# Rows of w_out kept in fours on a partition, and every fourth column of w_in as weights

## The chip, the cores and the metric

The kernel runs on one core of a Trainium2 chip. What counts is the device time of one execution in microseconds. The kernel before takes 178.99 us (median of three runs, 178.23 to 181.95).

## What is computed

A gated linear attention over 4 batches and 8 heads of 48 columns, 768 steps long, feeds a two-layer feed-forward block. Cut to what matters:

```python
f = 1.0 / (1.0 + np.exp(-f_logit))
for t in range(S):
    state = f[:, :, t, :, None] * state + np.einsum('bhd,bhe->bhde', k[:, :, t], v[:, :, t])
    y[:, :, t] = np.einsum('bhd,bhde->bhe', q[:, :, t], state)
x = y.transpose(0, 2, 1, 3).reshape(B * S, H * D)     # 3072 tokens of 384
h = x @ w_in                                          # 384 x 2048
g = h * (1.0 / (1.0 + np.exp(-h)))
out = g @ w_out                                       # 2048 x 384
```

All inputs and the output are float32. The sum over the 2048 columns of `h` may be taken in any order, as long as column f of `w_in` meets row f of `w_out`.

## The kernel before

The sequence is cut into chunks of 128 steps; two chunks (two batches, or two neighbouring chunks of one batch) form a pair, and there are 12 pairs. For each pair the kernel computes the attention inside the chunks and the running state in bfloat16, transposes the result into `xT` (384 rows on three blocks of 128 partitions, 256 tokens), and puts it through the block.

The first product (`mi`, L237 to L246) makes `h` with the hidden columns on partitions. One step `mi.P.j` fills one PSUM buffer of 128 x 512 with two blocks n = 2j and 2j+1 of 128 hidden columns for 256 tokens. Each block is three matmuls, one for each 128 rows of `w_in`: the weights are `w_in_sb[:, kk, n*128:(n+1)*128]`, 128 x 128, the moving operand is 256 columns of `xT`. A weight load and a matmul are two instructions on TensorE. In all L244 issues 576 pairs. The silu (`si`, L249, on ACT) writes the two blocks into `hT[:, 2j:2j+2, :]`. The second product (`mo`, L279) takes `hT[:, n, tokens]` as weights and `w_out_sb[:, n, :]` (384 columns) as the moving operand and sums over the 16 blocks n; `mo.P.i.s` does four of them. There are 384 such pairs.

Both weight matrices are loaded once, by four DMAs each, and turned to bfloat16 on the way (L197 to L206). They are issued by POOL, from its own queue. `wi.n` brings columns 512n to 512n+511 of `w_in`, that is blocks 4n to 4n+3, in rows of 2048 B. `wo.n` brings rows 512n to 512n+511 of `w_out`: partition p gets rows 512n + p, + 128, + 256 and + 384, each a row of 1536 B.

The order is written out by hand. `PLAN` lists every step with its engine and its buffers, and each engine runs its steps in that order; waits between engines, and between DMAs and engines, are put in by the framework, from the regions that an instruction reads and writes. The plan begins with `idle.512.10` and `idle.256.1`: ten matmuls of 512 columns and one of 256 that compute nothing (L424). The four w_in loads stand in the order `wi.1`, `wi.3`, `wi.0`, `wi.2`, then come `wo.0` to `wo.3`, each between other steps of POOL. The steps of TensorE around the first product's beginning, in order: `d.0` (L270), `mi.1.2`, `mi.1.3` (blocks 4 to 7), `y.0` (L258), `yi.0.1` (L352), `mi.1.6` (blocks 12, 13), `yT.0.0` and `yT.0.1` (L364), then 13 more `mi` steps of six matmuls, then the second product. The loads of q, k, v and f_logit, the DMA transposes and most stores are on SP's queue.

Of the kernel before, what the change touches and what calls it, by code (L numbers as in the profile page):

```python
# [106 lines left out]
def kernel(  # L107
# [10 lines left out]
    nc = tc.nc  # L118
# [8 lines left out]
    NT = d_ff // 128  # L127
# [28 lines left out]
    w_in_sb = sb.tile([128, KT, d_ff], BF16, name="w_in_sb")  # L156
    w_out_sb = sb.tile([128, NT, d_model], BF16, name="w_out_sb")
    w_in_src = moe_w_in.rearrange("(ko ki) n -> ki ko n", ki=128)
    w_out_src = moe_w_out.rearrange("(ko ki) n -> ki ko n", ki=128)
    SRC = {"f": f_logit, "k": k, "q": q, "v": v}  # L160

    plan = []
# [12 lines left out]
    at = lambda *key: where[key]  # L175
# [21 lines left out]
    def emit(kind, rest, eng):  # L197
        if kind in ("wi", "wo"):
            n, parts = rest[0], count[kind]
            if kind == "wi":  # L200
                w = d_ff // parts
                nc.gpsimd.dma_start(out=w_in_sb[:, :, n * w:(n + 1) * w], in_=w_in_src[:, :, n * w:(n + 1) * w])
            else:
                w = NT // parts
                nc.gpsimd.dma_start(out=w_out_sb[:, n * w:(n + 1) * w, :], in_=w_out_src[:, n * w:(n + 1) * w, :])
            return  # L206
        P = rest[0]
        form, *us = PAIRS[P]
        T = form == "T"
        if kind in SRC:  # L210
            j, parts = rest[1], count[kind, P]
            (b, c), (b1, c1) = us
            if T:
                h = H // parts
                w = h * 2 * D
                src = SRC[kind][b, j * h:(j + 1) * h, c * C:(c + 2) * C].rearrange("h (p t) d -> p h (t d)", t=2)
                dst = at(kind, P)[:, j * w:(j + 1) * w].rearrange("p (h w) -> p h w", h=h)
            else:
                n = 2 // parts
                w = n * HD  # L220
# [3 lines left out]
        if kind in "EL":  # L224
            j, parts = rest[1], count[kind, P]
            w = 2 * HD // parts
# [4 lines left out]
            if T:  # L231
                h = H // parts
                return nc.scalar.activation(lf.rearrange("p j h d -> p h j d")[:, j * h:(j + 1) * h, :, 0:D],
                                            e.rearrange("p (h j d) -> p h j d", j=2, d=D), AF.Ln, bias=1.0)
            n = 2 // parts
            return nc.scalar.activation(lf[:, j * n:(j + 1) * n, :, 0:D], e.rearrange("p (i h d) -> p i h d", i=n, d=D), AF.Ln, bias=1.0)
        if kind == "mi":  # L237
            j = rest[1]
            h = at("h", P, j).rearrange("p (n c) -> p n c", n=2)
            for i in range(2):  # L240
                n = 2 * j + i
                cols = slice(rest[2] * C, (rest[2] + 1) * C) if len(rest) > 2 else slice(0, 2 * C)
                for kk in range(KT):
                    nc.tensor.matmul(h[:, i, cols], w_in_sb[:, kk, n * 128:(n + 1) * 128], at("xT", P)[:, kk, cols],  # L244
                                     start=(kk == 0), stop=(kk == KT - 1))
            return  # L246
        if kind == "si":
# [25 lines left out]
        i = rest[1]  # L273
# [67 lines left out]
        elif kind == "at":  # L341
            r = rest[2]
# [78 lines left out]
    def run(kind, rest, eng, got):  # L421
        if kind == "idle":
            for _ in range(rest[1]):
                nc.tensor.matmul(buf["pb", int(got)][:, 0:rest[0]], triu, zero[:, 0:rest[0]], start=True, stop=True, skip_group_check=True)  # L424
            return
        slots = iter(got.split(",") if got else [])
        for key in takes(kind, rest):
            if key not in where:
                cls = cls_of(key[0])
                if cls == "st":  # L430
                    cls = f"st{PAIRS[key[1]][1 + key[2]][0]}"
                elif cls == "qkT" and len(key) == 2:
                    cls = "qkTT"
                where[key] = buf[cls, int(next(slots))]
        assert next(slots, None) is None, (kind, rest, got)
        emit(kind, rest, eng)
# [69 lines left out]
```

## Time and profile before

| | us |
|---|---|
| median of three runs | 178.99 (178.23 to 181.95) |
| the profiled execution | 178.94 |
| its span, first to last instruction | 177.2 |
| ACT's silu, L249, 96 of 610 ns | 50.5 busy |
| POOL's state update, L383, 40 of 543 ns | 21.7 busy |

The page counts an engine busy from the start of an instruction to its end; overlapping instructions are counted once. TensorE's matmuls are pipelined, so the spacing of their starts, and not the length of one, is what they cost in a stream. "PEld" are the weight loads, which overlap the matmuls. The granted clock, "PEclk", is 1.000 for the whole span. The 16 DMA engines moved 32.12 MB, at a mean of 181 GB/s; of the DMA engines' time SP's queue took 76.2% and POOL's 12.2%.

### The profile page before, as it was taken

What the parts mean: (1) busy time and instruction counts of PE and PEld (TensorE: products, weight loads), DVE (VectorE), ACT (ScalarE), POOL (GpSimd) and SP (SyncE); (2) the same over time, 40 slices, a digit from 0 to 9 for tenths busy, and PEclk for the clock granted to TensorE, in tenths of its full rate; (3) what the DMA queues carried; (4) which work ended last, traced back from release to release, by engine and by line L of the source; (5) the groups of instructions that cost most, each with busy time, mean ns of one, the idle gap of its engine ahead of it and who ended that gap; (6) DMA issues with size and microseconds to landing.
All of it is one profiled execution on the core that took longest, in us unless ns stands there. A gap on an engine that the chain in (4) does not pass through costs nothing.

```text
span 177.2 us, 4721 instructions
## 1 busy us (share of the span) xinstructions
PE 170.6 (96%) x1912; PEld 124.7 (70%) x1915; DVE 81.2 (46%) x165; ACT 130.4 (74%) x241; POOL 62.5 (35%) x105
## 2 busy tenths in 40 slices
PE   6998999999999999999999999999999999999991
PEld 2446688666886788766787687686797686877860
DVE  7089751047795783125777174035770152520110
ACT  3968578953999989998499788899589574281721
POOL 6056593102383348400647323400471960000001
PEclk9999999999999999999999999999999999999999
DMA  5999999999999989997698796899968998132202
GB/s 145 301 311 256 213 225 204 188 179 237 218 196 201 211 177 199 219 204 151 135 231 152 148 228 141 213 192 212 234 129 191 212 150 242 48 91 87 93 0 89
DMA packets 110453, 32.12 MB, mean 181 GB/s; under 512 B 104080, under 2 KB 110256, under 8 KB 110432
## 3 DMA queue, kind: packets, MB, share of 16 engines
q1 hardware_dynamic: 106432, 27.89, 76.2%
q0 software_dynamic: 4000, 3.93, 12.2%
q8 instruction: 15, 0.25, 0.6%
q14 instruction: 6, 0.05, 0.1%
HBM read 25.17 MB, written 4.72 MB: 169 GB/s over the span
## 4 chain that ended last, share of the span: by engine, by line
PE 74%; ACT 9%; DVE 6%; DMA 4%; SPq 3%; issue 2%; DVEq 0%; ACTq 0%
PE pb L279 32%; PE pb L244 27%; DVE qk L312 3%; DMA q<-in_q_dram 3%; ACT hT L249 3%; PE pb L340 2%; ACT L473 2%; ACT x L307 2%; PE pb L352 2%; PE pb L356 2%; PE pb L336 1%; SPq L368 1%; DMA out_dram<-ob 1%; SPq L223 1%; PE pb L364 1%
## 5 line engine op out<-in xcount | busy, mean ns | idle before, releaser
L244 PE MATMUL pb<-xT,w_in_sb 128*128 128x256 bf16 x576 | 69.3, 272 | 0.5 <-ACT ob L180 0.2
L279 PE MATMUL pb<-w_out_sb,hT 128*128 128x384 bf16 x384 | 68.5, 326 | 0.0
L244 PEld LDWEIGHTS <-w_in_sb 128*128 128x128 bf16 x576 | 54.9, 98 | 9.6 <-issue 1.2
L249 ACT ACTIVATE hT<-pb 128x512 bf16<-128x512 f32 x96 | 50.5, 610 | 10.7 <-PE pb L244 10.5
L279 PEld LDWEIGHTS <-hT 128*128 128x128 bf16 x384 | 36.2, 98 | 21.0
L383 POOL TENSOR_TENSOR st<-sd,al 48x192 bf16<-48x192 f32 x40 | 21.7, 543 | 56.8 <-PE pb L352 34.2
L344 DVE TENSOR_TENSOR atm<-pb,triu 128x512 bf16<-128x512 f32 x32 | 20.1, 684 | 11.2 <-PE pb L340 6.6
L307 ACT ACTIVATE x<-pb 128x384 f32<-128x384 f32 x48 | 21.1, 497 | 5.2 <-PE pb L295 3.1
L473 ACT ACT_TABLE_LOAD x17 | 21.8, 1283 | 0.3
L182 DVE COPY ob<-pb 128x384 f32<-128x384 f32 x10 | 5.4, 552 | 26.6 <-PE pb L279 26.6
L377 DVE TENSOR_TENSOR sd<-pb,st 128x384 f32<-128x384 f32 x16 | 8.8, 553 | 11.8 <-PE pb L373 10.3
L312 POOL TENSOR_TENSOR qk<-k,x 128x384 bf16<-128x384 f32 x11 | 12.0, 1102 | 5.5 <-ACT x L307 2.4
L312 POOL TENSOR_TENSOR qk<-q,x 128x384 bf16<-128x384 f32 x11 | 10.9, 997 | 8.5 <-ACT x L307 5.5
L229 ACT ACTIVATE e<-f 128x768 f32<-128x768 f32 (+1 forms) x13 | 10.2, 792 | 4.8 <-DMA f<-in_f_logit_dram 4.8
L180 ACT COPY ob<-pb 128x384 f32<-128x384 f32 x14 | 6.7, 482 | 9.0 <-PE pb L279 8.2
L312 DVE TENSOR_TENSOR qk<-q,x 128x384 bf16<-128x384 f32 x13 | 8.6, 682 | 7.7 <-DMA q<-in_q_dram 4.2
L289 POOL DMA_DIRECT2D out_dram<-ob x3 | 1.7, 562 | 28.5 <-DVE ob L182 28.5
L424 PE MATMUL pb<-zero,triu 128*128 128x512 bf16 (+1 forms) x27 | 9.8, 463 | 1.5 <-POOL triu masks.py:66 1.4
L344 DVE TENSOR_TENSOR atm<-pb,mask 128x512 bf16<-128x512 f32 x16 | 10.2, 684 | 2.1 <-PE pb L336 1.0
L182 POOL CAST vb<-v 128x384 bf16<-128x384 f32 x12 | 6.5, 551 | 10.9 <-DMA v<-in_v_dram 10.5
L182 DVE CAST yb<-pb 128x384 bf16<-128x384 f32 x14 | 7.6, 555 | 5.4 <-PE pb L356 2.8
L180 ACT CAST yb<-pb 128x384 bf16<-128x384 f32 x10 | 4.8, 490 | 5.8 <-PE pb L356 4.3
(71 smaller groups left out, 148.8 us busy)
## 6 DMA issues: line engine op xcount, KB each, us to landing
f<-in_f_logit_dram SPq DMA_DIRECT2D x11, 384.0 KB, 5.2
k<-in_k_dram SPq DMA_DIRECT2D x10, 384.0 KB, 5.2
q<-in_q_dram SPq DMA_DIRECT2D x10, 384.0 KB, 5.4
v<-in_v_dram SPq DMA_DIRECT2D x10, 384.0 KB, 5.3
out_dram<-ob SPq DMA_DIRECT2D x13, 192.0 KB, 2.1
w_in_sb<-in_moe_w_in_dram POOLq DMA_DIRECT2D x4, 384.0 KB, 8.4
w_out_sb<-in_moe_w_out_dram POOLq DMA_DIRECT2D x4, 384.0 KB, 10.3
out_dram<-ob SPq DMA_DIRECT2D x14, 96.0 KB, 3.5
```

Source lines behind the costliest of these rows:

```text
L180: nc.scalar.copy(dst, src)
L182: ENG[eng].tensor_copy(dst, src)
L229: return nc.scalar.activation(e, at("f", P)[:, j * w:(j + 1) * w], AF.Exp, scale=-1.0)
L244: nc.tensor.matmul(h[:, i, cols], w_in_sb[:, kk, n * 128:(n + 1) * 128], at("xT", P)[:, kk, cols], start=(kk == 0), stop=(kk == KT - 1))
L249: return nc.scalar.activation(at("hT", P)[:, 2 * j:2 * j + 2, :], at("h", P, j).rearrange("p (n c) -> p n c", n=2), AF.Silu)
L279: nc.tensor.matmul(o, at("hT", P)[:, n, i * C:(i + 1) * C], w_out_sb[:, n, :], start=(n == 0), stop=(n == NT - 1))
L307: nc.scalar.activation(at(kind, P, i).rearrange("p h d -> p (h d)"), at("cs", P, i)[:, 0:HD], AF.Exp, scale=1.0 if kind == "ia" else -1.0)
L312: ENG[eng].tensor_mul(at("qk", P, i)[:, j, :, 0:D], heads("qk"[j], P, i), at("ia" if j else "a", P, i))
L344: ENG[eng].tensor_mul(at("atm", P, i)[:, r], at(f"s{r}", P, i).rearrange("p (n c) -> p n c", c=C), mask[:, None, :].to_broadcast([C, NP, C]))
L383: nc.gpsimd.tensor_mul(at("st", P, i)[lo:lo + D, :, r * D:(r + 1) * D], at("sd", P, i)[lo:lo + D, :, r * D:(r + 1) * D], al_of(P, i)[lo:lo ...
L424: nc.tensor.matmul(buf["pb", int(got)][:, 0:rest[0]], triu, zero[:, 0:rest[0]], start=True, stop=True, skip_group_check=True)
L473: nc.scalar.preload_act_table_set(turns[n])
```

## The change

Partition p now holds four neighbouring rows of `w_out` for each quarter: rows 512m + 4p to 512m + 4p + 3, which lie together in memory and are loaded as one row of 6144 B. Place r of quarter m on partition p, `w_out_sb[p, 4m + r, :]`, is thus row 512m + 4p + r. For the first product to match, block n = 4m + r takes the columns 512m + 4p + r of `w_in`: every fourth column of a quarter, from the r-th on. `w_in` is loaded as before; the step of four is in the weight operand of the matmul.

```diff
-    w_out_src = moe_w_out.rearrange("(ko ki) n -> ki ko n", ki=128)
+    w_out_src = moe_w_out.rearrange("(m ki r) n -> m ki r n", ki=128, r=4)
...
-                w = NT // parts
-                nc.gpsimd.dma_start(out=w_out_sb[:, n * w:(n + 1) * w, :], in_=w_out_src[:, n * w:(n + 1) * w, :])
+                assert NT == 4 * parts
+                nc.gpsimd.dma_start(out=w_out_sb[:, 4 * n:4 * n + 4, :], in_=w_out_src[n])
...
                 n = 2 * j + i
+                m, r = n // 4, n % 4
                 cols = slice(rest[2] * C, (rest[2] + 1) * C) if len(rest) > 2 else slice(0, 2 * C)
                 for kk in range(KT):
-                    nc.tensor.matmul(h[:, i, cols], w_in_sb[:, kk, n * 128:(n + 1) * 128], at("xT", P)[:, kk, cols],
+                    nc.tensor.matmul(h[:, i, cols], w_in_sb[:, kk, 512 * m:512 * (m + 1)].rearrange("k (p r) -> k r p", r=4)[:, r], at("xT", P)[:, kk, cols],
                                      start=(kk == 0), stop=(kk == KT - 1))
```

One line is added ahead of the matmul, so that L244 is L245 after the change, and all later lines move by one.

## The prediction

> **What bounds the kernel now.** I read the page's head, busy times and chain first, to see which engine sets the end.
>
> ```profile
> span 177.2 us, 4721 instructions
> PE 170.6 (96%) x1912; PEld 124.7 (70%) x1915; DVE 81.2 (46%) x165; ACT 130.4 (74%) x241; POOL 62.5 (35%) x105
> PE 74%; ACT 9%; DVE 6%; DMA 4%; SPq 3%; issue 2%; DVEq 0%; ACTq 0%
> ```
>
> TensorE is busy for 96% of the span and carries 74% of the chain of waits. The timed run was 178.94 us, so 1.74 us lie outside the span; the median of the three runs, 178.99, is the same within 0.05. Busy time alone proves little for PE, because a matmul's recorded length is longer than its spacing. So I asked for the groups by line, then for the chain around the place where the first product begins.
>
> ```profile
> L244 PE MATMUL pb<-xT,w_in_sb 128*128 128x256 bf16 x576 | 69.3, 272 | 0.5 <-ACT ob L180 0.2
> L244 PEld LDWEIGHTS <-w_in_sb 128*128 128x128 bf16 x576 | 54.9, 98 | 9.6 <-issue 1.2
> ...
> L279 PE MATMUL pb<-w_out_sb,hT 128*128 128x384 bf16 x384 | 68.5, 326 | 0.0
> ```
>
> ```profile
> 20.17 1.42 PE pb L244 x12
> 21.59 0.51 PE pb L258 x32
> 22.09 0.28 PE pb L352 x4
> 22.37 0.65 PE pb L244 x6
> 23.02 0.34 PE pb L364 x6
> 23.36 8.52 PE pb L244 x78
> ```
>
> A first-product matmul is recorded at 272 ns, yet 78 of them take 8.52 us, 109 ns each. From 20.17 us the chain is PE piece on PE piece with no wait between them. The windows view says how much idle time PE has from there to the last matmuls:
>
> ```profile
> core 0: us, PE busy (x) PEld busy (x) DVE busy (x) ACT busy (x) POOL busy (x), PEclk, DMA share, GB/s
> 1.30:6.30 5.00, 4.93 (x12) 1.74 (x13) 2.81 (x21) 2.73 (x4) 2.16 (x13) 1.00 0.89 240
> ...
> 20.00:173.50 153.50, 152.97 (x1687) 115.11 (x1681) 67.52 (x122) 115.49 (x210) 53.04 (x78) 1.00 0.89 174
> ```
>
> Of 153.50 us, 152.97 are busy: 0.53 us of idle in all. Whatever holds PE after 20 us therefore comes out at the end, less 0.53 at most. The change has to be read for what it does to PE's stream.
>
> **The loads of w_out.** Four loads change from 512 rows of 1536 B each to 128 rows of 6144 B; bytes, queue and order stay. Before, from the page's list of DMA issues and from the timelines of POOL and PE:
>
> ```profile
> w_out_sb<-in_moe_w_out_dram POOLq DMA_DIRECT2D x4, 384.0 KB, 10.3
> ```
>
> ```profile
> 21.80 0.81 POOL L205 DMA_DIRECT2D w_out_sb<-in_moe_w_out_dram  x1
> ```
>
> ```profile
> 31.71 4.55 PE L279 MATMUL pb<-w_out_sb,hT 128*128 128x384 bf16 x27
> ```
>
> The typical load lands 10.3 us after its issue, and the first, issued at 21.80, would be there at about 32; the second product starts at 31.71 without a wait, so that one was a little quicker. No idle time on PE stands against these loads (0.0 in L279's row). If the long rows make them faster, the saving is bounded by nothing that waited: 0 us. If they make them slower, the cover is the delay of PE found below, some 9 us of further lead. I take 0. POOL issues the same eight weight loads, so its queue and SP's keep their order.
>
> **Every fourth column as weights.** The 576 weight loads of L244 now read 128 columns 8 B apart in place of 128 adjacent ones; count, destination and product stay. The trace has no weight load with a step, so the price is bounded. How fast can an adjacent one go? Where matmuls are short:
>
> ```profile
> 62.39 0.20 PE pb L356 x8
> ```
>
> Eight pairs of 128x128 load and 48-column matmul take 0.20 us, so such a load needs at most 25 ns, though its record, like L244's, says nearly 100: loads overlap. A load of L244 has the 109 ns of the matmul before it as cover. Reading four times the bytes to pick one column in four would make 4 x 25 = 100 ns, still 9 ns under the cover; below nothing it can't go, since PE is not waiting for weights now. So I take 0 for it, nearest to the covered row; the upper bound is in the rivals. [...]
>
> **A wait that the diff does not show.** The built program lists, ahead of the first two weight loads of L244 (L245 after the change), which semaphores they wait for. Before and after:
>
> ```
> L244 Ldweights w_in_sb [waits DMASW0_49]
> L244 Ldweights w_in_sb
> ...
> L245 Ldweights w_in_sb [waits DMASW2_49,DMASW0_49]
> L245 Ldweights w_in_sb [waits DMASW3_49,DMASW1_49]
> ```
>
> The four semaphores are the four w_in loads in the order of issue. Before, the first group waits for its own quarter alone, and the others are waited for by later groups. After, the stepped read is taken to overlap all quarters: the first group's first weight load waits for loads one and three, its second for two and four. When do they land? POOL's timeline has the issues, and the view of the tile the times to landing:
>
> ```profile
> 10.28 0.98 POOL L202 DMA_DIRECT2D w_in_sb<-in_moe_w_in_dram  x1
> ...
> 15.40 0.80 POOL L202 DMA_DIRECT2D w_in_sb<-in_moe_w_in_dram  x1
> ...
> 18.13 0.78 POOL L202 DMA_DIRECT2D w_in_sb<-in_moe_w_in_dram  x1
> ```
>
> ```profile
> DMA to landing us min/median/max: 7.1/8.4/8.8
> ```
>
> Asked for the fourth one alone (the issues between 18.0 and 18.3 us):
>
> ```profile
> w_in_sb<-in_moe_w_in_dram POOLq DMA_DIRECT2D x1, 384.0 KB, 8.7
> ```
>
> So the fourth load lands at 18.13 + 8.7 = 26.83 us, and the third at no later than 15.40 + 8.8 = 24.2. PE reaches the first group at 20.10:
>
> ```profile
> 20.10 1.21 PEld L244 LDWEIGHTS <-w_in_sb 128*128 128x128 bf16 x12
> ```
>
> It stands until about 24.2, does one matmul, and stands again until 26.83. The second load would have been at 20.10 + 0.11 = 20.21, so the delay is 26.83 - 20.21 = 6.62 us. The fourth load was issued before the hold began, and the w_out loads come behind it on its queue, so neither moves its landing much; if it landed as fast as the quickest of the four (7.1), the delay would be 5.0.
>
> Queued behind on PE, in the plan's order: the rest of that group, the next one, the 32 matmuls of y (L258), four of L352, another group, two transposes (L364), and the 78. For these wait ACT's and DVE's copies of y and of the transposed x, then every silu. All of it moves by 6.62 us, and there is nothing else that PE could do meanwhile, as its stream is in a fixed order. What can be won back is the 0.53 us of later idle; I take half, 0.27, since these waits end in work that itself comes from PE.
>
> **The half-speed stretch.** The kernel's first matmuls show what PE does out of a pause:
>
> ```profile
> 1.37 4.66 PE L424 MATMUL pb<-zero,triu 128*128 128x512 bf16 x11 [1.37 <-POOL triu masks.py:66]
> 6.03 0.71 PE L295 MATMUL pb<-lf,tincl 128*128 128x384 bf16 x2
> ...
> 7.32 0.59 PE L424 MATMUL pb<-zero,triu 128*128 128x512 bf16 x2
> 7.76 0.32 PE L295 MATMUL pb<-lf,tincl 128*128 128x384 bf16 x1
> ```
>
> Eleven idle matmuls (the plan's ten of 512 columns and one of 256, 10.5 x 512 together) take from 1.37 to 6.03, 4.66 us, 0.444 per 512. Two later ones start at 7.32 and are followed at 7.76: 0.22 per 512. PE begins at half speed, and the granted-clock column (1.00 between 1.30 and 6.30) does not show it. The stretch costs 4.66 - 10.5 x 0.22 = 2.35 us. From 20 us on the trace has no pause that would show whether one of 6.62 us, with one matmul in it, brings this state back. Bounds: 0, and twice 2.35 = 4.70 if coming back takes twice as long. I take 2.35, the one row there is. [...]
>
> **Sum.** 178.94 + 6.62 (wait) + 2.35 (half speed) - 0.27 (idle won back) + 0 (w_out rows) + 0 (stepped loads) = 187.6 us.
>
> **Rivals.** *The pause leaves the clock alone.* 178.94 + 6.62 - 0.27 = 185.3 us. For it: no row shows the state coming back. Against: PE stood before its first matmul too, and was slow. 18%.
>
> *The stepped weight load becomes PE's pace.* It decides from 109 ns per load, that is, at more than 4.4 times the 25 ns. At 5 times, 125 ns, each of the 576 costs 16 ns more, 9.2 us on top: 196.8. At 8 times, 200 ns, it is 91 ns and 52 us: 240. Against it speaks the wide cover; for it, that no stepped load stands in the trace. 14%, with 196.8 as its time.
>
> *The delay is given back, and the kernel isn't slower.* The chain has one place after 20 us where loads and stores carry it:
>
> ```profile
> 108.16 1.13 SPq L368
> ...
> 109.34 0.57 SPq L289
> ...
> 109.96 1.19 SPq L368
> ...
> 111.19 0.58 SPq L289
> ...
> 111.87 2.25 DMA out_dram<-ob
> ```
>
> Together these are 5.72 us. If the hold lets SP's queue run ahead so that all of it leaves the chain, and the clock stays up, the time is 178.94 + 6.62 - 5.72 = 179.8. It decides from PE idle time of at least 3 us to be had back, to stay within 2%. Against: the windows view has 0.53, as PE works through this stretch on other matmuls. 3%. A landing so early that the wait is not felt would need the fourth load 6 us sooner, ahead of anything that the change touches; I count it in here.
>
> **Numbers.** The forecast's chance is 62%; 3% are left for what I haven't thought of. The range: low is the quickest landing with no half speed and all idle time back, 178.94 + 5.02 - 0.53 = 183.4. High is 191.0, which takes in the doubled stretch (178.94 + 6.62 + 4.70 = 190.3) and a stepped load at up to 115 ns (187.6 + 576 x 0.006 = 191.1). That holds the first two cases, 80%. A measurement of this kernel can tell about 2% from no change, 3.6 us: slower takes the first three cases and most of the rest, 0.95; same 0.04; faster 0.01.
>
> **What would show it.** Right: a gap on PE from about 20.1 to 26.8 us, ended by the w_in loads, with one matmul near 24.2; matmuls of L245 spaced at about 218 ns for the first 3 to 5 us behind it and at 109 ns after that; nothing waiting for w_out; everything after 30 us moved by one amount. Wrong: no gap on PE there, or L245's matmuls over 109 ns throughout, or PE idle time elsewhere that shrinks by microseconds.

## The result and the profile after

The changed kernel takes 187.38 us (median of 6 runs, 186.63 to 189.04) beside 178.70 for the kernel before in the same runs: a ratio of 1.0498, with a 95% interval of 1.0445 to 1.0551. The profiled execution took 189.04 us, the longest of the six, with a span of 187.3. Here and below, the ratios leave out runs more than 1.5% above the fastest of their kernel.

The page after, in the order in which the page before was read (head, busy times, the clock by slices, chain, groups of the two products, queue 0, the w_out loads):

```profile
span 187.3 us, 4726 instructions
...
PE 172.9 (92%) x1915; PEld 132.2 (71%) x1915; DVE 83.5 (45%) x165; ACT 130.3 (70%) x241; POOL 62.3 (33%) x105
...
PEclk9999955999999999999999999999999999999999
...
q0 software_dynamic: 2464, 3.93, 11.0%
...
PE 73%; DMA 12%; ACT 8%; SPq 2%; issue 1%; DVE 1%; POOL 0%; POOLq 0%; ACTq 0%
...
L245 PE MATMUL pb<-xT,w_in_sb 128*128 128x256 bf16 x576 | 71.2, 277 | 8.0 <-DMA w_in_sb<-in_moe_w_in_dram 7.6
L245 PEld LDWEIGHTS <-w_in_sb 128*128 128x128 bf16 x576 | 62.2, 114 | 11.8 <-issue 8.6
L280 PE MATMUL pb<-w_out_sb,hT 128*128 128x384 bf16 x384 | 68.5, 326 | 0.0
...
w_out_sb<-in_moe_w_out_dram POOLq DMA_DIRECT2D x4, 384.0 KB, 6.4
```

Three things are new. The first product has 7.6 us of idle time ended by the w_in loads, where it had 0.5 in all. The chain has 12% DMA in place of 4%. And the clock has two slices at 5 tenths, right behind. The second product's row is the one of before to the digit. A mean weight load of the first product is recorded at 114 ns in place of 98.

PE's timeline at that place, before and after (start, length, what; the bracket gives the idle time ahead and what ended it):

```profile
19.66 0.51 PE L270 MATMUL pb<-vb,qk 64*128 64x96 bf16 x16
20.10 1.48 PE L244 MATMUL pb<-xT,w_in_sb 128*128 128x256 bf16 x12
...
23.20 8.68 PE L244 MATMUL pb<-xT,w_in_sb 128*128 128x256 bf16 x78
```

```profile
20.15 0.52 PE L271 MATMUL pb<-vb,qk 64*128 64x96 bf16 x16
26.09 0.38 PE L245 MATMUL pb<-xT,w_in_sb 128*128 128x256 bf16 x1 [5.43 <-DMA w_in_sb<-in_moe_w_in_dram]
28.68 2.51 PE L245 MATMUL pb<-xT,w_in_sb 128*128 128x256 bf16 x11 [2.21 <-DMA w_in_sb<-in_moe_w_in_dram]
...
33.72 8.68 PE L245 MATMUL pb<-xT,w_in_sb 128*128 128x256 bf16 x78
```

One matmul, a second pause, and then eleven that take 2.51 us: less the 0.42 that one of them is long, ten spacings of 0.21 us, twice the 109 ns of before. The 78 behind take 8.68 us in both. By the start of the 78 the program is 10.52 us late (33.72 - 23.20), and that divides like this: PE arrives 0.49 us later (20.15 against 19.66); the second matmul is at 28.68 instead of 20.10 + 0.11 = 20.21, which leaves 28.68 - 20.21 - 0.49 = 7.98 us of pause; the stretch from there to the 78 takes 5.04 us in place of 2.99, so 2.05 us go to half speed. The span grew by 10.1 us: all of it arises in these 14 us, and 0.4 us come back later. The windows view shows the clock there (its last columns are granted clock, DMA share, GB/s):

```profile
21.00:23.00 2.00, 0.00 (x0) 0.00 (x0) 1.39 (x3) 0.16 (x1) 1.55 (x3) 1.00 1.20 204
23.00:25.00 2.00, 0.00 (x0) 0.00 (x0) 0.00 (x0) 0.00 (x0) 0.00 (x0) 0.51 1.21 201
...
32.00:33.00 1.00, 1.00 (x8) 0.78 (x8) 0.56 (x1) 0.48 (x1) 0.50 (x1) 0.50 0.75 158
33.00:36.00 3.00, 3.00 (x31) 2.84 (x29) 2.08 (x3) 2.22 (x3) 2.88 (x5) 0.95 0.79 128
```

The clock falls to half near 23.0 us, some 2.4 us into the pause, and is back at about 33.3 (0.95 over 33 to 36 is 0.3 us at half).

Why was the pause longer than 6.62 us here? POOL's timeline after:

```profile
19.66 0.50 POOL L182 CAST vb<-v 128x384 bf16<-128x384 f32 x1 [3.04 <-DMA v<-in_v_dram]
20.10 0.78 POOL L202 DMA_DIRECT2D w_in_sb<-in_moe_w_in_dram  x1
```

POOL casts v before it issues the fourth w_in load, and in this execution v came later, so the load was issued at 20.10 us instead of 18.13. It landed 8.4 us after that. The 18.13 was one value of several: in the other profiles with this order of loads the fourth issue stands between 17.48 us (the first experiment) and 20.53 us (the changed kernel run again).

### The profile page after: what moved, and what is told of

Its sections match the earlier page's. It is cut to its first block, busy times and chain, and to the rows that moved or that the text cites. A ratio compares the mean times of both kernels' runs of the same rounds, so it can differ in the third digit from the quotient of the medians.

```text
span 187.3 us, 4726 instructions
## 1 busy us (share of the span) xinstructions
PE 172.9 (92%) x1915; PEld 132.2 (71%) x1915; DVE 83.5 (45%) x165; ACT 130.3 (70%) x241; POOL 62.3 (33%) x105
## 4 chain that ended last, share of the span: by engine, by line
PE 73%; DMA 12%; ACT 8%; SPq 2%; issue 1%; DVE 1%; POOL 0%; POOLq 0%; ACTq 0%
PE pb L280 33%; PE pb L245 28%; DMA v<-in_v_dram 5%; DMA w_in_sb<-in_moe_w_in_dram 5%; ACT hT L250 2%; DMA f<-in_f_logit_dram 2%; PE pb L341 2%; ACT L474 2%; ACT x L308 2%; PE pb L353 2%; SPq L223 2%; PE pb L357 2%; PE pb L303 1%; PE pb L374 1%; PE pb L365 1%
## 5 line engine op out<-in xcount | busy, mean ns | idle before, releaser
L245 PE MATMUL pb<-xT,w_in_sb 128*128 128x256 bf16 x576 | 71.2, 277 | 8.0 <-DMA w_in_sb<-in_moe_w_in_dram 7.6
L245 PEld LDWEIGHTS <-w_in_sb 128*128 128x128 bf16 x576 | 62.2, 114 | 11.8 <-issue 8.6
L280 PE MATMUL pb<-w_out_sb,hT 128*128 128x384 bf16 x384 | 68.5, 326 | 0.0
L250 ACT ACTIVATE hT<-pb 128x512 bf16<-128x512 f32 x96 | 50.5, 611 | 10.8 <-PE pb L245 10.5
L280 PEld LDWEIGHTS <-hT 128*128 128x128 bf16 x384 | 36.2, 98 | 20.8
L313 POOL TENSOR_TENSOR qk<-k,x 128x384 bf16<-128x384 f32 x11 | 12.5, 1147 | 5.4 <-ACT x L308 2.2
L229 ACT ACTIVATE e<-f 128x768 f32<-128x768 f32 (+1 forms) x13 | 10.2, 789 | 3.4 <-DMA f<-in_f_logit_dram 3.4
L425 PE MATMUL pb<-zero,triu 128*128 128x512 bf16 (+1 forms) x30 | 10.3, 455 | 1.4 <-POOL triu masks.py:66 1.4
L345 DVE TENSOR_TENSOR atm<-pb,mask 128x512 bf16<-128x512 f32 x16 | 10.2, 682 | 2.1 <-PE pb L337 1.0
L313 DVE TENSOR_TENSOR qk<-k,x 128x384 bf16<-128x384 f32 x13 | 10.1, 793 | 0.0
```

The lines of the kernel that those rows point to most:

```text
L229: return nc.scalar.activation(e, at("f", P)[:, j * w:(j + 1) * w], AF.Exp, scale=-1.0)
L245: nc.tensor.matmul(h[:, i, cols], w_in_sb[:, kk, 512 * m:512 * (m + 1)].rearrange("k (p r) -> k r p", r=4)[:, r], at("xT", P)[:, kk, cols] ...
L250: return nc.scalar.activation(at("hT", P)[:, 2 * j:2 * j + 2, :], at("h", P, j).rearrange("p (n c) -> p n c", n=2), AF.Silu)
L280: nc.tensor.matmul(o, at("hT", P)[:, n, i * C:(i + 1) * C], w_out_sb[:, n, :], start=(n == 0), stop=(n == NT - 1))
L313: ENG[eng].tensor_mul(at("qk", P, i)[:, j, :, 0:D], heads("qk"[j], P, i), at("ia" if j else "a", P, i))
L345: ENG[eng].tensor_mul(at("atm", P, i)[:, r], at(f"s{r}", P, i).rearrange("p (n c) -> p n c", c=C), mask[:, None, :].to_broadcast([C, NP, C]))
```

## The experiments

All ratios are to the kernel before on the same chip. The experiments ran in three sets on three chips (the first three below and the run with 28 idle matmuls; the changed kernel run again, the run with 24 and the two with short matmuls; the wait for the third load and the early loads). The kernel before took from 178.2 to 183.8 us there, so ratios are compared, not times.

**The long rows of w_out alone.** Adjacent columns again, w_out as changed:

```diff
-nc.tensor.matmul(h[:, i, cols], w_in_sb[:, kk, 512 * m:512 * (m + 1)].rearrange("k (p r) -> k r p", r=4)[:, r], ...
+nc.tensor.matmul(h[:, i, cols], w_in_sb[:, kk, n * 128:(n + 1) * 128], ...
```

> The four-row partitions of w_out alone; the first product takes adjacent columns as before, so column f of w_in meets another row of w_out. Theory (the whole loss is the early wait and the half-speed stretch behind it): no gap at 20 us, the time of before, 178.7 us within 1. If the long w_out rows cost PE or the other loads something: over 180.5 us. If they gain: the w_out loads land in about 6 us in place of 10, and the time is under 177.9; theory says that they land sooner and that nothing comes of it.

The ratio is 1.0008 (0.9975 to 1.0040): no change. The view of the tile w_out_sb says how soon the loads were there:

```profile
DMA to landing us min/median/max: 7.3/8.2/10.4
```

That is 2.1 us sooner at the median than before (10.3), in one execution each, less than the 4 us expected; in the profile of the changed kernel the first load, issued in the pause, took 8.4 us too, and only the three issued behind the pause were faster (5.3 to 7.2 us). Nothing comes of it, as no instruction waited for them.

**The whole change without the overlap.** Four tiles for w_in:

```diff
-    w_in_sb = sb.tile([128, KT, d_ff], BF16, name="w_in_sb")
+    w_in_q = [sb.tile([128, KT, d_ff // 4], BF16, name=f"w_in_q{m}") for m in range(4)]
...
-nc.gpsimd.dma_start(out=w_in_sb[:, :, n * w:(n + 1) * w], ...
+nc.gpsimd.dma_start(out=w_in_q[n], ...
...
-w_in_sb[:, kk, 512 * m:512 * (m + 1)].rearrange("k (p r) -> k r p", r=4)[:, r]
+w_in_q[m][:, kk].rearrange("k (p r) -> k r p", r=4)[:, r]
```

> The whole change, but with the four quarters of w_in in four tiles, so that a stepped read can overlap its own quarter alone. Theory: the first group waits for its quarter alone, no gap, no half speed; 178.7 us within 1. If the stepped weight loads are part of the loss, the kernel keeps that part: spacing of the first product's matmuls over 109 ns, or over 180.5 us in all.

1.0017 (0.9980 to 1.0055), 12 runs: the loss is gone with every other part of the change in place. PE's timeline and the group of its weight loads:

```profile
19.88 1.50 PE L245 MATMUL pb<-xT,w_in_q 128*128 128x256 bf16 x12
...
23.00 8.68 PE L245 MATMUL pb<-xT,w_in_q 128*128 128x256 bf16 x78
```

```profile
L245 PEld LDWEIGHTS <-w_in_q 128*128 128x128 bf16 x576 | 61.6, 114 | 4.1 <-issue 1.4
```

No pause, and 78 matmuls in the same 8.68 us, although a stepped load's record is 114 ns here too.

**The wait alone.** The kernel before, with one more matmul ahead of the first group; it reads the quarter that is loaded last:

```diff
             h = at("h", P, j).rearrange("p (n c) -> p n c", n=2)
+            if (P, j) == (1, 2):
+                nc.tensor.matmul(h[:, 0, 0:64], triu, w_in_sb[:, 0, 1024:1088], start=True, stop=True, skip_group_check=True)
```

> The kernel before, nothing of the change, with one 64-column matmul that reads the last-loaded quarter of w_in put ahead of the first group; what it writes is overwritten. It makes PE wait for all four loads. Theory: a gap from 20.2 to about 26.8 us and 4 to 5 us at half speed behind it; 187.4 us within 1, the time of the changed kernel. If the stepped loads or the w_out rows carry part of the loss, it stays below that: at 185 or less.

1.0522 (1.0468 to 1.0577), a median of 188.0 us: the whole loss of the change, with nothing of the change in the kernel. PE's timeline:

```profile
26.89 0.23 PE L241 MATMUL pb<-w_in_sb,triu 128*128 128x64 bf16 x1 [6.58 <-DMA w_in_sb<-in_moe_w_in_dram]
26.94 2.75 PE L246 MATMUL pb<-xT,w_in_sb 128*128 128x256 bf16 x12
29.62 0.82 PE L260 MATMUL pb<-vb,atm 64*128 64x48 bf16 x32
...
32.26 0.93 PE L246 MATMUL pb<-xT,w_in_sb 128*128 128x256 bf16 x7
```

A pause of 6.58 us, and twelve matmuls of the first product in 2.68 us up to the next line, 0.22 each. The last row is the beginning of the 78 (the view ends there): from the twelve to it 5.32 us, in place of 3.10 before.

**The same with a shorter wait.** The extra matmul reads the quarter loaded third (`w_in_sb[:, 0, 0:64]` in the line above):

> As the run with the wait alone (the kernel before, one extra 64-column matmul ahead of the first group), but it reads the quarter that is loaded third, which lands near 24.2 us. The pause is 3.9 us in place of 6.6. If half speed comes only with a pause of some 5 us or more: 179 + 3.9 = 183 us, granted clock 1.0 throughout. If it comes with this pause too: 179 + 3.9 + about 2.3 = 185 us, a stretch at 0.5 behind the pause.

1.0268 (1.0163 to 1.0372), a median of 185.12 us. The pause in the profile is 5.20 us in place of the 3.9 expected, as the third load landed at about 25.7 us in this execution; the first twelve matmuls are at half speed again, the next lines at full speed:

```profile
25.79 0.23 PE L241 MATMUL pb<-w_in_sb,triu 128*128 128x64 bf16 x1 [5.20 <-DMA w_in_sb<-in_moe_w_in_dram]
25.84 2.75 PE L246 MATMUL pb<-xT,w_in_sb 128*128 128x256 bf16 x12
28.52 0.60 PE L260 MATMUL pb<-vb,atm 64*128 64x48 bf16 x32
...
29.23 0.82 PE L246 MATMUL pb<-xT,w_in_sb 128*128 128x256 bf16 x6
...
30.23 5.95 PE L246 MATMUL pb<-xT,w_in_sb 128*128 128x256 bf16 x53
```

So half speed came with this pause too. The loss is smaller than with the wait for the fourth load for two reasons in the profiles: the pause is 1.4 us shorter, and from the twelve matmuls to the 78 it is 4.39 us in place of 5.32, as full speed came back sooner. By how much at the end, two chips and one profile each don't settle. The pause of 3.9 us that the run was to try did not come about.

**PE kept busy in the pause.** Idle matmuls in the plan of the changed kernel, ahead of the first group, 28 of them and in a later run 24:

```diff
-mi.1.2:P:7
+idle.512.28::7 mi.1.2:P:7
```

> The changed kernel with 28 idle matmuls of 512 columns (28 x 0.215 = 6.0 us) ahead of the first group, so that PE works through most of the wait. Theory: the wait stays, the half-speed stretch goes: matmuls of the first product at 109 ns from the first on, granted clock 1.0 there, 187.4 - 2.3 = 185.1 us within 0.7. If the stretch costs nothing, the time stays at 187.4; if the idle matmuls outlast the wait, up to 0.5 us more.

> The changed kernel with 24 idle matmuls of 512 columns (5.2 us) in the hold, four fewer than in the run before, which came out slower than the changed kernel although its first product ran at full speed at once. If the half-speed stretch is worth its 2.3 us at the end: 2.3 us under the changed kernel on the same chip. If what is won there is lost again at a later wait on SP's transposes (one profile shows 1.6 us at the scores of the last pairs, about 159 us): within 1 us of the changed kernel, with a wait of L341 for qkT between 140 and 165 us that the changed kernel does not have.

> The changed kernel itself, on the same chip as the next run, to compare with. 187.4 us within 1.5; a gap from about 20.3 us until the fourth w_in load, 4 to 5 us at half speed behind it.

With 28 the ratio is 1.0603 (1.0544 to 1.0661), worse than the changed kernel, against the expectation. With 24 it is 1.0420 (1.0347 to 1.0493; from four of its six runs), beside 1.0521 (1.0483 to 1.0558) for the changed kernel in the same set of runs; the medians of all six runs of each are 187.49 and 188.41 us. What the idle matmuls were meant to do at the place, they did. PE's timelines of the changed kernel run again and of the one with 28:

```profile
24.24 0.38 PE L245 MATMUL pb<-xT,w_in_sb 128*128 128x256 bf16 x1 [3.15 <-DMA w_in_sb<-in_moe_w_in_dram]
28.17 2.51 PE L245 MATMUL pb<-xT,w_in_sb 128*128 128x256 bf16 x11 [3.55 <-DMA w_in_sb<-in_moe_w_in_dram]
...
32.42 0.82 PE L245 MATMUL pb<-xT,w_in_sb 128*128 128x256 bf16 x6
```

```profile
28.55 1.36 PE L245 MATMUL pb<-xT,w_in_sb 128*128 128x256 bf16 x11 [1.19 <-DMA w_in_sb<-in_moe_w_in_dram]
...
31.53 1.69 PE L245 MATMUL pb<-xT,w_in_sb 128*128 128x256 bf16 x14
```

Eleven matmuls in 1.36 in place of 2.51 us. From the second matmul to the last row it is 2.98 us with the idle matmuls and 4.25 without: 1.27 us won at once. In both profiles with idle matmuls, 28 and 24, about as much is lost again near 160 us, where PE waits for a DMA transpose (the waits of PE, the same row in both):

```profile
PE pb L341 <- DMA qkT<-qk: 1.4, 1, 1.4
```

Neither profile of the changed kernel has such a row. The profiled execution with 24 is its longest, 188.78 us; the shorter ones, down to 185.29, have no profile, so whether they lack the wait is not known. With 24 the end got 1.0% of 179, 1.8 us, with intervals that just overlap. So the half-speed stretch is plain in the trace, but its worth at the end is settled only to lie between nothing and about 2 us.

Why 28 came out worse than 24 stays open. Three of its four runs (189.26 to 190.31 us) show a mean granted clock of 0.991, so a part of each ran at a lower clock; the profiled one, at 1.000, took 188.44 and doesn't show where. That mark is not the idle matmuls' own: the longest run of the kernel before has it in each set (183.83, 183.61 and 183.49 us).

**What a stepped weight load costs by itself.** With four tiles, the first product's matmuls were cut to 64 columns, four times as many, so that the matmul covers some 27 ns of a load (an estimate, a quarter of the 109) in place of 109; once with adjacent columns (and `w_out` as before), once with the step (and `w_out` as changed). `W` stands for the weights:

```diff
-                for kk in range(KT):
-                    nc.tensor.matmul(h[:, i, cols], W, at("xT", P)[:, kk, cols], ...
+                for c0 in range(0, 2 * C, 64):
+                    for kk in range(KT):
+                        nc.tensor.matmul(h[:, i, c0:c0 + 64], W, at("xT", P)[:, kk, c0:c0 + 64], ...
```

> Adjacent columns as weights, four tiles for w_in, w_out as before, the first product cut into matmuls of 64 columns, four times as many (2304), so that a weight load has 27 ns of matmul as cover in place of 109. Spacing of the first product's matmuls 27 to 30 ns, as 25 ns are seen with 48 columns; the kernel within 10 us of 179.

> The same with every fourth column as weights (the whole change, four tiles). If a stepped load costs no more than an adjacent one: the spacing of the run before, 27 to 30 ns. If its longer record (113 in place of 98 ns) is time of the load itself: about 40 to 45 ns, some 30 us more in all. If four times the bytes are read one after the other: 100 ns.

PE's timelines, one undisturbed row of each:

```profile
25.51 3.89 PE L245 MATMUL pb<-xT,w_in_q 128*128 128x64 bf16 x128 [1.75 <-issue]
```

```profile
26.30 4.42 PE L246 MATMUL pb<-xT,w_in_q 128*128 128x64 bf16 x128 [1.65 <-issue]
```

Less the last matmul's own length (194 and 198 ns by the groups) that is 3.70 and 4.22 us for 127 spacings: 29 ns with adjacent and 33 ns with stepped columns. The step adds 4 ns to the spacing there, neither the 15 ns of the longer record nor a multiple; by that estimate 27 ns of each load are still covered by a matmul, so what the step costs below that is not shown. (One run each. Both kernels also have idle time on PE for which the profile shows no cause, "issue" in the rows, 5.6 and 3.1 us ahead of the first product's matmuls in all, so their times, 192.8 and 196.9 us, say less; the first is outside the 10 us around 179 that were expected.)

**The loads earlier.** The changed kernel with `wi.1 wi.3 wi.0 wi.2` ahead of POOL's first cast, `vb.1.0`, in the plan:

> The changed kernel with all four w_in loads issued by POOL right behind its masks, at about 4 us, ahead of its first cast. They have landed before PE comes to the first product, so the wait on all four is there but isn't felt: no pause, clock 1.0. What it costs: they compete with the first loads of f, k, q and v, which set the pace of the first 10 us. If that competition is dear, PE comes to the first product several us after 20.2, and the time is 183 us or more; if it is cheap, 179 to 181.

1.0416 (1.0305 to 1.0527), a median of 187.64 us. The wait is gone and another has come. POOL's and PE's timelines:

```profile
3.99 3.24 POOL L202 DMA_DIRECT2D w_in_sb<-in_moe_w_in_dram  x4
18.66 0.68 POOL L182 CAST vb<-v 128x384 bf16<-128x384 f32 x1 [11.43 <-DMA v<-in_v_dram]
```

```profile
19.39 0.83 PE L271 MATMUL pb<-vb,qk 64*128 64x96 bf16 x16 [6.66 <-POOL vb L182]
...
29.86 1.50 PE L245 MATMUL pb<-xT,w_in_sb 128*128 128x256 bf16 x12
```

The first v pays for the early weights: issued at 4.2 us as before, it landed after 14.3 us in place of 5.3, and its cast starts at 18.66 us in place of 9.61. PE stands for 6.66 us at another place, with half speed behind it (the sixteen matmuls of L271 take 0.83 us; in the timeline of the changed kernel 0.52). The first product starts 10 us late, though without a wait of its own.

## Why the prediction was right

*PE's stream decides.* Right: 10.5 us lost by 33.7 us came out as 10.1 us at the end. What came back, 0.4 us, is under the bound of 0.53.

*The hidden wait.* Right in kind and place: one matmul between two pauses, both ended by w_in loads. Shown by taking it away (four tiles: 1.0017) and by putting it alone into the kernel before (1.0522, beside the change's 1.0498 and 1.0521). Its size varies with the execution: 6.6 us forecast and seen in the run with the wait alone, but 7.98 in the profile after and 7.05 when the changed kernel ran again (28.17 less 20.21, less the 0.91 that PE came later). The term took the fourth load's issue as fixed, since it stands ahead of the pause; but it stands behind a cast that waits for v, and moved by 2 us.

*Half speed.* Right in kind, and with it falls the rival by which the pause leaves the clock alone. Its size was taken too high: 2.35 us forecast, 2.05 measured in the profile after, and 1.26 when the changed kernel ran again (4.25 in place of 2.99 us from the second matmul to the 78). The forecast took the one row of the kernel's start; in the profile after the same eleven idle matmuls take 4.66 us as well, but 4.08 in the run with the wait for the third load and 4.07 in the one with the early loads, a loss of 1.8 (4.07 - 10.5 x 0.22), so that row was at the upper end of these four. One remark of the prediction has to be narrowed, that the granted-clock column does not show the state. It does not for the first microseconds, where it says 1.00 over matmuls at half speed (0.444 us per 512 columns in place of 0.22); here, in the middle of the span, it shows 0.50. So the column tells, in steps of 0.1 us of the windows view, when the clock fell and came back in four profiles:

| profile | fell, us after the pause began | back, us after the last wait ended | half speed in all, us | loss behind the pause, us |
|---|---|---|---|---|
| the change | 2.4 | 4.6 | 10.2 | 2.05 |
| the change again | 3.1 | 2.8 | 6.8 | 1.26 |
| the wait alone | 1.3 | 5.0 | 10.2 | 2.2 |
| the wait for the third load | 1.2 | 2.8 | 6.8 | 1.3 |

The clock neither fell at one length of the pause nor came back at one distance behind it: it fell 1.2 to 3.1 us into the pause and came back 2.8 to 5.0 us after its end. The stretch lasted 6.8 or 10.2 us in all, and a little under half of its part behind the pause was lost.

*The rows of w_out.* Right at 0. The working missed that PE's pause holds up POOL as well: its state update stands for 9.60 us until PE's L353, and the last three w_out loads come behind it, the second at 33.50 in place of 23.70 us. They still land in time, as L280's 0.0 shows.

*Stepped weight loads.* Right at 0: with four tiles the 78 matmuls take the same 8.68 us, and the spacing of 33 ns lies far under the 109 that cover it; the bound of 100 ns was three times too high.

*The delay given back.* Fell: the changed kernel kept all but 0.4 us.

The mechanism was forecast, but that 187.6 us came within 0.3 of the measured 187.38 is luck. In the two profiles of the changed kernel the pause is 1.4 and 0.4 us over its term, PE arrives 0.5 and 0.9 us late, which no term held, and half speed is 0.3 and 1.1 us under its term: the errors partly cancel. The profiled execution of the result is also 1.7 us over the median, so its terms add up to more than the typical run lost.

## What to carry to other kernels

The framework can take an operand read with a step to overlap regions that it doesn't touch, as it did here: look at the waits of the built program, not only at the diff, and give each load that is waited for by itself a tile of its own (1.0017 here in place of 1.0498). PE issues in a fixed order and had 0.53 us of slack: of a delay of 10.5 us it kept 10.1. In the four profiles above a pause of 5 to 8 us cost 1.3 to 2.2 us more at half speed behind it. Rows that loaded faster, 8.2 us at the median in place of 10.3, were worth nothing, as no instruction waited for them (1.0008).

## What the runs showed of the hardware

A 128 x 128 bfloat16 weight load with a step of four columns is recorded at 114 ns in place of 98, yet under matmuls of 64 columns the loads follow each other every 33 ns in place of 29: the record of a load said little here of what it costs in a stream. And with the four w_in loads issued by POOL from 3.99 us on, in place of 10.70, the first v on SP's queue landed 14.3 us after its issue in place of 5.3; PE stood for 6.66 us until the cast of v, about as long as the wait that the early loads were to remove.
